# Attention's output with its tokens on the partitions, in the banks of the scores

## The chip, the cores and the metric

One core of a Trainium2 chip. The metric is the time of one execution on the device, in microseconds (us). Engines: TensorE (PE in the profile, PEld its weight loads), VectorE (DVE), ScalarE (ACT), GpSimd (POOL), SyncE (SP), which issues the DMAs here.

## The reference

```python
# q, k, v, f_logit: (4, 8, 768, 48)
f = 1.0 / (1.0 + np.exp(-f_logit))
for t in range(S):
    state = f[:, :, t, :, None] * state + np.einsum('bhd,bhe->bhde', k[:, :, t], v[:, :, t])
    y[:, :, t] = np.einsum('bhd,bhde->bhe', q[:, :, t], state)
x = y.transpose(0, 2, 1, 3).reshape(B, S, H * D)              # (4, 768, 384)
xn = (x - mean(x)) / np.sqrt(var(x) + 1e-06) * g_ln
x = x + np.maximum(xn @ w_ch1, 0.0) @ w_ch2                    # first MLP, 384 - 1536 - 384
h = np.maximum(x.transpose(0, 2, 1) @ w_tok1, 0.0) @ w_tok2    # token mixing, 768 - 256 - 768
u = x + h.transpose(0, 2, 1)
out = u + np.maximum(u @ w_ch1b, 0.0) @ w_ch2b                 # second MLP
```

## The kernel before

Attention with a gate per channel is cut into 24 units: unit n is chunk c = n // 4 (128 tokens) of batch b = n % 4. Gates become cumulated logs (`clamp`, `log`, `scan`), with which k and q are scaled (`ek`, `eq`, `km`, `qm`). A chunk is two halves of 64 tokens (index i), its 8 heads are 4 pairs (index p) of two (index r): head (p, r) has its 48 channels on partitions 64r to 64r + 47 of the tiles K and Q. Most of a unit's products use a quarter of TensorE's array (64 rows by 64 columns). All of them are fp32, and each shows in the trace as two instructions.

The steps of a unit, by their names in the order list:
- `kp` transposes K (4 transposes), `kt` copies it out.
- `sc` (L331): 16 score products (p, r, i), into two PSUM banks, one for each r. `st` (L344): 16 statistics products (new state of each half), into other columns of the same two banks.
- `A0`, `A1` (L354): VectorE masks the scores of r = 0 and r = 1 into A.
- `stm`, `ste`, `std`: state at the middle and the end of the chunk, and its decay.
- `y` (L399): output products that go to PSUM bank k from row half k of the array: 8 `carried(0)` products (old state by Q, first half; only if c > 0) and 8 `inner(0)` (V by A). `yw` (L409): a one-element VectorE memset that waits for the last of `y`. `z` (L416): 8 `inner(1)` and 8 `carried(1)`, whose first waits for that memset, since now the other row half writes each bank. The result `yT` has channels on partitions and tokens along the row.
- `yc0`, `yc1` (L423): ScalarE copies the two banks out. `yt` (L433): 4 transposes turn the output to tokens on partitions.
- `lna`, `lnc`, `lnv`, `lnr`: layer norm from those (`lna` ScalarE, copy with row sums; `lnc` VectorE, centred and scaled xn).
- `tp`: 3 transposes of xn; `ah` (ScalarE) and `al` (VectorE) split them in two fp32r parts.

The first MLP (`mlp`) works in 8 steps of 3 units. `m<step>.<f>` is a first-layer product group (9 products of 128x128 by 384 columns, three terms of a split), `h` (ScalarE) and `l` (VectorE) bring its hidden part out, `o<u><g>` is a second-layer group of 9 products, `r` adds the result to x. Nine such products are a slot. Step s begins at slot 29 + 24 s. Unit n (from 3 on) is placed at s0 = 22 + 8 (n - 3), so one unit goes with eight slots. Steps `w..` convert the first MLP's weights (`a`, `b`, `c` VectorE, `h` ScalarE, `l` VectorE or GpSimd), `s..` those of later stages.

What sets the order: each engine runs its instructions in the order in which they are emitted. Everything due before slot 77 is emitted in the order written out in `ORDER` ("+k" puts k small products on zeros in front, to keep the clock up), the rest sorted by due time, at equal times engines first and TensorE's pieces last, attention before the MLP. `POOL` names the steps that go to GpSimd in place of VectorE; from unit 12 on all that can go there do.

PSUM before: `scp` two banks (scores of one unit), `atp` three (kp, yT, y, tp), `mmp` three (first and second layer products).

Of the kernel before, what the change touches and what calls it, by code (L numbers as in the profile page):

```python
# [7 lines left out]
F32 = mybir.dt.float32  # L8
# [10 lines left out]
DM = H * D  # L19
# [27 lines left out]
    w3.l 2.qm 3.km 3.qm w12.l 1.std 4.qm w14.l w4.l w1.l w5.l 6.km w13.l w17.l w15.l 2.std 5.std 4.std 7.km 3.std  # L47
    w6.l 8.km 8.qm 9.qm w19.l w23.l 11.km 11.qm 11.std
""".split())
ORDER = """  # L50
    0.lf 1.lf 0.clamp 0.log 3.lf w3.ld 4.lf 1.clamp 3.clamp 0.scan 1.log 2.lf 3.log 0.lq 1.lq 1.scan w3.a 2.clamp
    4.clamp 1.ek 3.scan 0.eq 0.lv 0.ek 4.log w12.ld 0.km 2.log w3.b 0.kp+31 0.qm 1.km 0.sc+7 2.scan 0.kt 3.eq
    w14.ld w3.c w3.h 0.st 4.scan 0.A0 0.y+21 w2.ld 1.kp 2.ek 1.eq 1.kt 1.tot 4.ek 0.stm 0.A1 w12.a 0.ste 0.yw 1.lv
    w14.a 1.qm 2.lq 0.tot w3.l w14.b 0.z 0.yc0 1.sc+4 3.tot 2.eq 0.yc1 2.tot 2.qm w12.b 1.st w2.a 2.km 2.kp+5 2.kt
    1.A1 1.A0 1.stm 1.ste w14.c 1.y+3 3.lq 2.lv 0.yt 4.lq 3.ek 3.km 0.lna 5.lf w2.b 2.sc 1.yw 3.lv 0.lnc w2.c
    w0.ld 1.z 2.st 1.yc0 3.qm 2.A1 2.A0 4.tot 0.tp w5.ld 2.stm w4.ld 1.yc1 3.kp 0.ah 3.kt 4.eq 4.lv 0.al w2.h
    2.ste w12.c 2.y+9 6.lf 2.yw 1.yt w2.l 5.clamp 4.km 1.lna w13.ld w12.h 3.sc w1.ld 2.z 2.yc0 5.log 3.st 1.lnc
    w12.l 3.A1 3.A0 1.tp+7 1.std 3.stm 4.qm 2.yc1 4.kp 2.yt 1.ah 5.scan 4.kt 1.al 2.lna 2.lnc 3.ste 3.y+14 3.yw
    2.tp 0.lnv 1.lnv 2.ah 3.z w4.a w0.a 6.clamp w4.b 3.yc0 3.yc1 2.al 4.sc 4.st 3.yt 5.lq w4.c 0.std 5.ek w0.b
    m0.3 4.A0 w14.h 3.lna w14.l 4.y 4.A1 4.stm 6.lv w15.ld m0.2 w4.h w0.c 3.lnc 4.ste 6.log 4.yw w0.h w4.l 2.lnv  # L60
    3.tp 5.eq w1.a w5.a 4.z w1.b 5.km 5.lv w1.c w1.h 4.yc0 m0.h2 m0.h3 5.qm w7.ld m0.4 w17.ld 5.kp 6.scan 5.sc
    4.yc1 m0.l2 w1.l 5.kt m0.l3 4.yt 5.st m0.1 6.tot 4.lna 6.lq w5.b w13.a w5.c w0.l 5.tot w13.b 4.lnc 5.A0 w13.c
    3.ah w5.h m0.0 m0.h4 6.ek m0.h0 5.y m0.l4 5.stm m0.h1 w5.l m0.5 5.A1 w13.h w17.a w11.ld w16.ld 7.lf 5.yw m0.l0
    m0.l1 6.eq w15.a 6.km 5.z 6.qm w15.b 5.ste w13.l w17.b 8.lf 8.lv w16.a 5.yc0 m0.h5 5.yc1 3.lnv m0.o00 w16.b
    7.lq 6.kp 4.tp 6.sc 6.kt w17.c w17.h w15.c 5.yt 6.st m0.o10 w16.c 5.lna m0.l5 6.A1 7.clamp w15.h m0.o20 5.lnc
    w17.l w10.ld w16.h 4.ah 5.tp w16.l w15.l w6.ld m0.o11 m0.o21 5.ah 2.lnr 4.al w6.a 5.al 6.A0 2.std 6.y 7.log
    6.stm 7.scan m0.o01 w19.ld 7.ek m0.r21 8.clamp 6.yw 3.al 5.std w10.a 7.tot m0.r11 w10.b m1.2 w7.a 4.std m1.5
    6.ste w7.b 8.log m0.r01 5.lnv 7.eq 6.z m1.h2 7.km w10.c w7.c 9.lf w6.b m1.l2 w6.c 7.qm m1.1 m1.h1 4.lnv m1.h5
# [12 lines left out]
    10.qm 10.kt 11.lq s2.ld 10.sc m1.d0 m0.r23 s0.a 9.yt 10.st m0.o02 11.ek m1.o13 11.eq m0.o03 m0.o12 10.stm
    m1.r13 s1.b 9.std s0.b 10.A1 10.ste 10.A0 7.std m1.d1 m1.o22 10.std m0.d2 m0.o13 m0.r03 m0.r13 s0.c m0.d1 s1.c
    m0.d0 m1.o23 9.lna 8.lnr s0.h 8.std
# [71 lines left out]
def head(p, r):  # L155

    return 4 * (p // 2) + 2 * r + p % 2


def main_path(ctx, tc, q_t, k_t, f_t, v_n, g_rep, w1, w2, wt1, wt2, w3, w4, out, x1_d, f_d, h_d, t_d):  # L160
# [71 lines left out]
    atp = at.enter_context(tc.tile_pool(name="atp", bufs=3, space=PSUM))  # L232
# [17 lines left out]
    def attention(n):  # L250
# [80 lines left out]
        def scores(z=0):  # L331

            t["sc"] = [scp.tile([128, 512], F32, tag="sc", name="sc") for _ in range(2)]
            busy(t["sc"][0], z)
            for p in range(NP):
                for r in range(2):
                    for i in range(2):
                        nc.tensor.matmul(t["sc"][r][half(i), HC * p:HC * p + HC], t["K"][rows(r), p, half(i)],  # L338
                                         t["Q"][rows(r), p, half(i)])

        def new(i):
            return t["sc"][i][:P2, NP * HC:NP * HC + NP * D]

        def stat():  # L344
            for p in range(NP):
                for i in range(1 if last else 2):
                    for r in range(2):
                        h, w = head(p, r), width(r)
                        o = NP * HC + D * p
                        nc.tensor.matmul(t["sc"][i][64 * r:64 * r + w, o:o + D],  # L350
# [3 lines left out]
        def scores_e(g):  # L354
            a = s2.tile([128, NP, HC], F32, tag=f"A{g}", name=f"A{g}")
            t["A", g] = a
            nc.vector.tensor_tensor(
                a, t["sc"][g][:, :NP * HC].rearrange("p (a c) -> p a c", a=NP),
                upper.rearrange("p (o c) -> p o c", o=1).to_broadcast([128, NP, HC]), op=ALU.mult)
# [20 lines left out]
        def carried(i):  # L380
# [18 lines left out]
        def outp(z=0):  # L399
# [4 lines left out]
            if c:  # L404
                carried(0)
# [10 lines left out]
        def outp2():  # L416
# [3 lines left out]
            carried(1)  # L420
            follow(block.instructions[z], t["done"])

        def outp_e(k):  # L423


            if not k:
# [920 lines left out]
```

## Time and profile before

| | us |
|---|---|
| median of 3 runs | 772.51 (771.8 to 772.72) |
| the profiled execution | 774.89 |
| its span, first to last instruction | 773.1 |
| TensorE busy | 758.7 (98%) |
| VectorE busy | 519.3 (67%) |
| ScalarE busy | 370.4 (48%) |
| GpSimd busy | 147.7 (19%) |
| moved by DMA | 120.18 MB, 155 GB/s |

The granted clock of TensorE is 0.995 of full speed over the span. The start is the attention of the first units and the conversion of weights; from about 41 us the first MLP runs, mixed with attention to about 382 us; then token mixing and the second MLP.

### The profile page before, as it was taken

The numbers are of one execution on the slowest core, as the hardware profiler recorded it, in microseconds if no ns is written. First come the engines' busy times: TensorE is split into PE (matmuls) and PEld (weight loads), VectorE is DVE, ScalarE is ACT, GpSimd is POOL, SyncE is SP. The second block draws the span as 40 slices with busy tenths as digits, with TensorE's granted clock in tenths as the row PEclk, the third lists the DMA queues.
The fourth block names the chain that finished last, engine by engine and source line by source line (L and its number), as shares of the span: only waits on it lengthen the run. The fifth ranks groups of instructions, "written<-read, shape, count | busy, mean of one in ns | idle before, by whom it ended". The sixth has DMA issues, their size and how long they took to land.

```text
span 773.1 us, 17492 instructions
## 1 busy us (share of the span) xinstructions
PE 758.7 (98%) x7110; PEld 735.6 (95%) x7110; DVE 519.3 (67%) x969; ACT 370.4 (48%) x899; POOL 147.7 (19%) x119
## 2 busy tenths in 40 slices
PE   8899999999999999999999999999999999999996
PEld 7799999999999999999999999999999999999996
DVE  7798886687785867555344664877558664868481
ACT  6675454363644645444131442664247442656440
POOL 1344212145343333230000010101001010101010
PEclk9999999999999999999999999999999999999998
DMA  9674342465566555652347984345343544343401
GB/s 264 188 212 157 115 151 68 146 191 193 181 220 171 157 166 171 192 176 84 102 140 272 341 299 139 97 138 170 95 130 93 178 127 137 96 143 100 132 21 67
DMA packets 61001, 120.18 MB, mean 155 GB/s; under 512 B 6896, under 2 KB 29040, under 8 KB 60144
## 3 DMA queue, kind: packets, MB, share of 16 engines
q1 hardware_dynamic: 60912, 118.98, 49.1%
q8 instruction: 58, 0.95, 0.5%
q14 instruction: 31, 0.25, 0.1%
HBM read 94.57 MB, written 24.38 MB: 154 GB/s over the span
## 4 chain that ended last, share of the span: by engine, by line
PE 90%; DMA 3%; DVE 2%; issue 2%; POOL 1%; SPq 1%; ACT 1%; POOLq 0%
PE mo L945 19%; PE mo L576 18%; PE mm L546 18%; PE mm L892 17%; PE rt L812 3%; PE ht L834 3%; PE yT L396 2%; DMA first<-in_q_t 2%; PE yT L387 2%; PE sc L338 2%; PE sc L350 1%; PE y L439 1%; PE tp L510 1%; DMA ts<-t_d 1%; PE kp L315 1%
## 5 line engine op out<-in xcount | busy, mean ns | idle before, releaser
L546 PE MATMUL mm<-wx 128*128 128x384 f32 x864 | 163.2, 340 | 0.4 <-DVE hl L565 0.4
L546 PEld LDWEIGHTS mm<-wx 128*128 128x128 f32 x864 | 148.5, 188 | 2.5 <-DVE hl L565 1.1
L892 PE MATMUL mm<-xsh,wx 128*128 128x384 f32 x528 | 137.9, 334 | 0.9 <-DVE q L908 0.9
L576 PE MATMUL mo<-w2h,hh 128*128 128x384 f32 x288 | 101.1, 351 | 0.2 <-DVE hl L565 0.2
L945 PE MATMUL mo<-w2h,hh 128*128 128x384 f32 x288 | 97.0, 337 | 0.0
L892 PEld LDWEIGHTS mm<-xsh,wx 128*128 128x128 f32 x528 | 95.6, 188 | 1.3 <-PE mm L892 1.2
L576 PE MATMUL mo<-w2h,hl 128*128 128x384 f32 x288 | 96.6, 335 | 0.0
L576 PE MATMUL mo<-w2l,hh 128*128 128x384 f32 x288 | 96.4, 335 | 0.0
L945 PE MATMUL mo<-w2h,hl 128*128 128x384 f32 x288 | 96.3, 334 | 0.0
L945 PE MATMUL mo<-w2l,hh 128*128 128x384 f32 x288 | 96.2, 334 | 0.0
L932 POOL TENSOR_TENSOR hl<-u,hh 128x768 fp32r<-128x768 f32 x16 | 29.7, 1854 | 337.9 <-ACT u L927 244.0
L892 PE MATMUL mm<-xsl,wx 128*128 128x384 f32 x264 | 88.2, 334 | 0.0
L561 ACT ACTIVATE hh<-mm 128x384 fp32r<-128x384 f32 x96 | 46.3, 487 | 62.3 <-PE mm L546 61.7
L565 DVE SCALAR_TENSOR_TENSOR hl<-mm,hh 128x384 fp32r<-128x384 f32 x96 | 52.5, 551 | 22.8 <-ACT hh L561 22.1
L949 DVE TENSOR_TENSOR xr<-mo,xr 128x384 f32<-128x384 f32 x48 | 26.6, 555 | 53.5 <-PE mo L945 53.5
L1103 ACT ACTIVATE cs<-cs 128x384 f32<-128x384 f32 x56 | 31.1, 555 | 59.2 <-DVE cs L1100 59.0
L576 PEld LDWEIGHTS mo<-w2h,hh 128*128 128x128 f32 x288 | 54.1, 188 | 1.9 <-DVE hl L565 0.3
L576 PEld LDWEIGHTS mo<-w2l,hh 128*128 128x128 f32 x288 | 54.2, 188 | 0.0
L945 PEld LDWEIGHTS mo<-w2h,hh 128*128 128x128 f32 x288 | 54.1, 188 | 0.1
L945 PEld LDWEIGHTS mo<-w2l,hh 128*128 128x128 f32 x288 | 54.1, 188 | 0.0
L945 PEld LDWEIGHTS mo<-w2h,hl 128*128 128x128 f32 x288 | 54.1, 188 | 0.0
L576 PEld LDWEIGHTS mo<-w2h,hl 128*128 128x128 f32 x288 | 54.0, 188 | 0.0
(163 smaller groups left out, 1372.7 us busy)
## 6 DMA issues: line engine op xcount, KB each, us to landing
cs<-in_w SPq DMA_DIRECT2D x48, 384.0 KB, 3.3
sg<-in_w SPq DMA_DIRECT2D x44, 384.0 KB, 4.5
ts<-t_d SPq DMA_DIRECT2D x48, 256.0 KB, 2.9
wx<-f_d SPq DMA_DIRECT2D x6, 1152.0 KB, 12.4
F<-in_f_t SPq DMA_DIRECT2D x21, 224.0 KB, 3.9
T<-in_k_t SPq DMA_DIRECT2D x21, 224.0 KB, 3.3
T<-in_q_t SPq DMA_DIRECT2D x21, 224.0 KB, 4.2
x_d<-x SPq DMA_DIRECT2D x24, 192.0 KB, 2.6
```

The lines of the kernel that those rows point to most:

```text
L338: nc.tensor.matmul(t["sc"][r][half(i), HC * p:HC * p + HC], t["K"][rows(r), p, half(i)], t["Q"][rows(r), p, half(i)])
L546: nc.tensor.matmul(ps, w[:, f, k, :], x[:, k, :], start=(i == 0), stop=(i == 8))
L561: nc.scalar.activation(out=hid(f)[0], in_=t[f], func=AF.Relu)
L565: nc.vector.scalar_tensor_tensor(hl, t[f], 0.0, hh.bitcast(F32), op0=ALU.max, op1=ALU.subtract)
L576: nc.tensor.matmul(ps, x, w[:, f, :], start=(f == lo and i == 0), stop=(f == hi and i == 2))
L812: nc.tensor.matmul(t["r"][j], w, x, start=(s == 0 and i == 0), stop=(s == NCH - 1 and i == 2))
L834: nc.tensor.matmul(ps, w, x[:, j], start=(i == 0), stop=(i == 5))
L892: nc.tensor.matmul(ps, w, x, start=n == 0, stop=n == len(ops) - 1)
L932: le.tensor_tensor(l, whole(g, i), h.bitcast(F32), op=ALU.subtract)
L945: nc.tensor.matmul(ps, x, w[:, f], start=(g % 3 == 0 and m == 0 and n == 0), stop=(g % 3 == 2 and m == 1 and n == 2))
L949: nc.vector.tensor_tensor(us[b, u], t["o", u], us[b, u], op=ALU.add)
L1103: nc.scalar.activation(out=t["u"], in_=t["u"], func=AF.Abs, accum_out=wlow[:, i:i + 1])
```

## The change

The heads are paired anew (head (p, r) = 4 r + p), and the output is made with A or Q as the stationary operand and V or the state as the streamed one, so that tokens come out on partitions. It is written into the columns of the unit's own score banks that the scores have left. Bank r then holds the 192 channels of heads 4r to 4r + 3. `yc0`, `yc1` and `yt` go; `lna` and `lnc` read the score banks. For r = 1 the token halves of A are swapped, so V is also loaded with swapped halves (W, half a V more for each unit). `y` is now the 16 inner products, `z` the carried ones behind the memset. The score tile is two banks, two deep; `atp` has one bank (kp); `tp` goes to `mmp`. `ORDER` and `POOL` are written anew.

```diff
 def head(p, r):
-    return 4 * (p // 2) + 2 * r + p % 2
+    return NP * r + p
...
-    atp = at.enter_context(tc.tile_pool(name="atp", bufs=3, space=PSUM))
+    atp = at.enter_context(tc.tile_pool(name="atp", bufs=1, space=PSUM))
...
-                t["V"] = vp.tile([128, DM], F32, tag="V", name="V")
-            nc.sync.dma_start(out=t["V"], in_=v_n[n])
+                v = vp.tile([128, DM + DM // 2], F32, tag="V", name="V")
+                t["V"], t["W"] = v[:, :DM], v[:, DM:]
+                nc.sync.dma_start(out=v, in_=v_n[n])
...
-            t["sc"] = [scp.tile([128, 512], F32, tag="sc", name="sc") for _ in range(2)]
-            busy(t["sc"][0], z)
+            t["sc"] = scp.tile([128, 2, 512], F32, tag="sc", name="sc")
+            busy(t["sc"][:, 0], z)
...
-                        nc.tensor.matmul(t["sc"][r][half(i), HC * p:HC * p + HC], t["K"][rows(r), p, half(i)],
+                        nc.tensor.matmul(t["sc"][half(i ^ r), r, HC * p:HC * p + HC], t["K"][rows(r), p, half(i)],
                                          t["Q"][rows(r), p, half(i)])
...
-                    o = slice(64 * (p % 2), 64 * (p % 2) + width(p % 2))
-                    nc.tensor.matmul(t["yT"][r ^ i][o, r, p // 2], s[rows(r), D * p:D * p + width(p % 2)],
-                                     t["Q"][rows(r), p, half(i)], start=(i == 0 and p < 2),
-                                     stop=(i == 1 and p > 1))
-
-        def inner(r):
+                    nc.tensor.matmul(t["sc"][half(i), r, D * p:D * p + D], t["Q"][rows(r), p, half(i)],
+                                     s[rows(r), D * p:D * p + D], start=False, stop=p == NP - 1)
+
+        def inner():
             for p in range(NP):
-                for i in range(2):
-                    h = head(p, r)
-                    o = slice(64 * (p % 2), 64 * (p % 2) + width(p % 2))
-                    nc.tensor.matmul(t["yT"][r ^ i][o, r, p // 2], t["V"][half(i), D * h:D * h + width(p % 2)],
-                                     t["A", r][half(i), p], start=(c == 0 and r == 0 and p < 2), stop=False)
+                for r in range(2):
+                    for i in range(2):
+                        k = half(i ^ r)
+                        o = D * p
+                        nc.tensor.matmul(t["sc"][half(i), r, D * p:D * p + D], t[r][k, p],
+                                         t["W" if r else "V"][k, o:o + D], start=p == 0,
+                                         stop=p == NP - 1 and c == 0 and i == 0)
...
-            if c:
-                carried(0)
-            inner(0)
+            inner()
             t["half"] = nc.cur_bb.bb.instructions[-1]
...
-            inner(1)
+            if c:
+                carried(0)
             carried(1)
             follow(block.instructions[z], t["done"])
...
-            xn, g = (a.rearrange("p (i a c) -> p i a c", i=4, a=2) for a in (t["xn"], gln))
-            y = t["y"].rearrange("p (i a c) -> p i a c", i=4, a=2)[..., :D]
-            nc.vector.scalar_tensor_tensor(xn, y, t["nm"][:, 0:1], g, op0=ALU.add, op1=ALU.mult)
+            nc.vector.scalar_tensor_tensor(heads(t["xn"]), y(), t["nm"][:, 0:1], heads(gln), op0=ALU.add, op1=ALU.mult)
...
-                (-6, sl.e, ktrans_e, "kt"), (-4.7, sl.p, scores, "sc"), (-4.7, sl.p, stat, "st"),
-                (-4, sl.e, lambda: scores_e(0), "A0"), (-4, sl.e, lambda: scores_e(1), "A1"),
+                (-6, sl.e, ktrans_e, "kt"), (-4.9, sl.p, scores, "sc"), (-4.89, sl.p, stat, "st"),
+                (-4, sl.e, (lambda: scores_e(0)) if n < 11 else scores_e2, "A0"),
+                (-4, sl.e, (lambda: scores_e(1)) if n < 11 else None, "A1"),
...
-                (3, sl.p, outp, "y"), (3.05, sl.e, outp_w, "yw"), (3.2, sl.p, outp2, "z"),
-                (4, sl.e, lambda: outp_e(0), "yc0"), (4, sl.e, lambda: outp_e(1), "yc1"),
-                (5, sl.p, outp_t, "yt"), (6, sl.e, ln_a, "lna"), (7, sl.e, ln_c, "lnc"), (11.1, sl.p, trans, "tp"),
+                (3.01, sl.p, outp, "y"), (3.05, sl.e, outp_w, "yw"), (3.2, sl.p, outp2, "z"),
+                (4.2, sl.e, ln_a, "lna"), (5, sl.e, ln_c, "lnc"), (11.3, sl.p, trans, "tp"),
...
-        ps = atp.tile([128, 512], F32, tag="at", name="tp")
+        ps = mmp.tile([128, 512], F32, tag="mm", name="tp")
```

TensorE's pieces in the two hand-written lists, from unit 4's `y` on ([k] is k groups of nine large products; before it, units 0 to 3 go to `z` and the scores and statistics of unit 4 are done in both; before also has `3.yt`):

```
before: 4.y [1] 3.tp 4.z [1] 5.kp 5.sc 4.yt 5.st [2] 5.y [1] 5.z [1] 6.kp 4.tp 6.sc 5.yt 6.st [2] 5.tp [2] 6.y [3]
        6.z [2] 7.kp [1] 7.sc [1] 7.st [3] 6.yt [2] 8.kp [1] 7.y [1] 8.sc [1] 8.st [1] 7.z [1] 8.y [3] 7.yt 8.z [2]
        6.tp 9.kp [2] 8.yt 7.tp [1] 8.tp 9.sc [1] 9.st [2] 9.y [1] 10.kp 9.z [1] 10.sc 9.yt 10.st [7]
after:  4.y [2] 4.z [2] 5.kp [1] 5.sc 5.st 3.tp 6.kp 4.tp 5.y 6.sc [1] 6.st [2] 5.z [2] 5.tp 6.y [4] 6.z [1] 7.kp
        [1] 7.sc [2] 7.st [4] 7.y [5] 7.z [1] 8.sc [3] 8.kp [2] 8.st 9.kp [1] 6.tp [1] 8.y [1] 8.z 9.sc [1] 7.tp 9.st
        [2] 9.y [1] 8.tp 10.kp 10.sc 9.z [2] 10.st [5]
```

In front of the first large product the new list has these more on VectorE: two weight steps `a`, two `b`, one `c`, both masks of unit 4, two products `qm`; and these less: one `std`, one `l`.

## Rows read from the trace of the kernel before

**Rows 1.** Busy time by stretch, from and to in us.

```profile
142.00:388.00 246.00, 245.41 (x2934) 235.65 (x2933) 168.23 (x332) 117.19 (x291) 79.46 (x61) 1.00 0.54 169
...
424.00:773.00 349.00, 341.80 (x1990) 340.14 (x1988) 223.59 (x366) 165.06 (x392) 29.66 (x16) 0.99 0.45 140
```

The columns are length, then busy us (and instructions) of PE, PEld, DVE, ACT, POOL, then TensorE's granted clock, DMA share and GB/s.

**Rows 2.** TensorE's waits over the span: us in total, times, longest.

```profile
PE sc L338 <- issue: 3.0, 2, 1.6
...
PE mm L546 <- DVE hl L565: 0.4, 1, 0.4
```

**Rows 3.** The chain that ended last: start us, us, what.

```profile
40.85 1.58 PE mm L546 x9
```

**Rows 4.** Busy time by stretch, the start; columns as in rows 1.

```profile
0.00:25.00 25.00, 20.77 (x349) 18.00 (x350) 18.90 (x43) 15.93 (x33) 5.77 (x12) 1.00 0.86 239
25.00:50.00 25.00, 22.90 (x533) 20.36 (x533) 20.76 (x48) 17.68 (x51) 8.10 (x7) 0.93 0.66 210
```

**Rows 5.** Timeline of TensorE, 262 to 290 us: start us, us, what.

```profile
261.67 2.07 PE L546 MATMUL mm<-wx 128*128 128x384 f32 x11
263.67 0.45 PE L387 MATMUL yT<-T,state 48*64 48x64 f32 x16
263.94 0.41 PE L396 MATMUL yT<-A,V 64*48 64x64 f32 x16
264.28 0.45 PE L576 MATMUL mo<-w2h,hh 128*128 128x384 f32 x1
264.57 0.34 PE L576 MATMUL mo<-w2l,hh 128*128 128x384 f32 x1
...
265.78 0.34 PE L576 MATMUL mo<-w2h,hl 128*128 128x384 f32 x1
265.96 0.49 PE L510 MATMUL tp<-ident,xn 128*128 128x128 f32 x3
266.38 0.45 PE L396 MATMUL yT<-A,V 64*64 64x64 f32 x16
266.65 0.41 PE L387 MATMUL yT<-T,mid 48*48 48x64 f32 x16
266.88 0.65 PE L338 MATMUL sc<-T 48*64 48x64 f32 x32
267.34 0.64 PE L350 MATMUL sc<-V,kt 64*48 64x48 f32 x32
267.91 0.44 PE L576 MATMUL mo<-w2h,hh 128*128 128x384 f32 x1
268.19 0.33 PE L576 MATMUL mo<-w2l,hh 128*128 128x384 f32 x1
...
269.60 0.55 PE L439 MATMUL y<-ident,ys 112*128 112x112 f32 x4
269.92 0.42 PE L576 MATMUL mo<-w2h,hh 128*128 128x384 f32 x1
270.17 0.34 PE L576 MATMUL mo<-w2l,hh 128*128 128x384 f32 x1
```

**Rows 6.** The output's transposes, 56 to 390 us: duration ns min/median/max, first and last start.

```profile
L439 PE MATMUL y<-ident,ys x76: 257/259/316, 59.1 to 365.7; 112*128 112x112 f32 x76
```

**Rows 7.** Statistics instructions begun by 267.68 us, by shape: xcount, busy us, mean ns.

```profile
L350 PE MATMUL sc<-V,kt 64*48 64x48 f32 x16 | 0.5, 206 | 0.0
L350 PE MATMUL sc<-V,kt 64*64 64x48 f32 x12 | 0.5, 216 | 0.0
```

**Rows 8.** The copies of xn's transposes, 56 to 390 us, columns as in rows 6.

```profile
L532 DVE TENSOR_TENSOR wx<-tp,wx x21: 544/548/557, 62.4 to 377.8; 128x384 fp32r<-128x384 f32 x21
L528 ACT ACTIVATE wx<-tp x20: 470/491/498, 61.3 to 377.3; 128x384 fp32r<-128x384 f32 x20
```

**Rows 9.** Timeline of VectorE, 195 to 217 us; idle before, in brackets.

```profile
201.98 0.75 DVE L357 TENSOR_TENSOR A<-sc,upper 128x256 f32<-128x256 f32 x2 [2.89 <-PE sc L350]
...
212.47 1.47 DVE L633 TENSOR_TENSOR sg<-cu,sg 128x256 fp32r<-128x256 f32 x1
```

More of the change, by code (lines that the diff above doesn't have):

```diff
@@ L52 @@
[L52 to L56, printed above, removed]
@@ L349, in stat, with scores_e, scores_e2 @@
                         o = NP * HC + D * p
[L350 removed]
+                        nc.tensor.matmul(t["sc"][64 * r:64 * r + w, i, o:o + D],
                                          t["kt"][half(i), P2 * p + 64 * r:P2 * p + 64 * r + w],
                                          t["V"][half(i), D * h:D * h + D])
[L354 to L356 removed]
+        def scores_e(g, gs=None):
+            if g not in t:
+                t["A"] = s2.tile([128, 2, NP, HC], F32, tag="A", name="A")
+                t[0], t[1] = t["A"][:, 0], t["A"][:, 1]
+            g = slice(g, g + 1) if gs is None else gs
+            w = g.stop - g.start
             nc.vector.tensor_tensor(
[L358 to L359 removed]
+                t["A"][:, g], t["sc"][:, g, :NP * HC].rearrange("p r (a c) -> p r a c", a=NP),
+                upper.rearrange("p (r a c) -> p r a c", r=1, a=1).to_broadcast([128, w, NP, HC]), op=ALU.mult)
+        def scores_e2():
+            scores_e(0, slice(0, 2))
         def old():
@@ L418, in outp2, with heads, y @@
             z = len(block.instructions)
-            inner(1)
+            if c:
+                carried(0)
             carried(1)
             follow(block.instructions[z], t["done"])
-        def outp_e(k):
-            if not k:
-                t["yf"] = s1.tile([P2, 10, HC], F32, tag="ys", name="ys")
-                t["ys"] = t["yf"][:, :8].rearrange("p (r g i) c -> p r g (i c)", r=2, g=2)
-            to = t["yf"].rearrange("p (r x) c -> p r x c", r=2)[:, :, 0:3:2] if not k else \
-                t["yf"][:, 1:7].rearrange("p (r x) c -> p r x c", r=2)[:, :, 0:3:2]
-            nc.scalar.activation(out=to, in_=t["yT"][k][:P2], func=AF.Copy)
-        def outp_t(z=0):
-            t["y"] = atp.tile([128, 512], F32, tag="at", name="y")
-            busy(t["y"], z)
-            for g in range(2):
-                for r in range(2):
-                    i = 128 * (2 * g + r)
-                    nc.tensor.matmul(t["y"][:, i:i + P2], t["ys"][:, r, g], ident[:P2, :P2], is_transpose=True)
+        def heads(x):
+            return x.rearrange("p (r c) -> p r c", r=2)
+        def y():
+            return t["sc"][:, :, :DM // 2]
         def ln_a():
@@ L1185, in general_path @@
                         nc.vector.tensor_copy(ya[:, :, :, e], ps)
-                    nc.sync.dma_start(
-                        out=x_d[b].rearrange("c t (p e) -> t c p e", p=NP)[:, :, bass.ds(p, 1), :].rearrange(
-                            "t c p e -> t c (p e)"),
-                        in_=ya.rearrange("t c r e -> t c (r e)"))
+                    for r in range(2):
+                        nc.sync.dma_start(
+                            out=x_d[b].rearrange("c t (h e) -> t c h e", h=H)[:, :, bass.ds(p + NP * r, 1), :].rearrange(
+                                "t c h e -> t c (h e)"),
+                            in_=ya[:, :, r])
         with tc.tile_pool(name="gw", bufs=1) as gw, tc.tile_pool(name="gx", bufs=2) as gx, \
```

84 lines of the change are left out of this document (45 added, 39 removed).

## The prediction

> **What bounds the kernel now.** I read the table of stretches first. From 142 to 388 us, where attention and the first MLP run mixed, TensorE is busy 245.41 of 246 us; behind 424 us it is 341.80 of 349 [rows 1]. VectorE is at 168 of 246 there, ScalarE at 117, the DMA share is 0.54. Then the waits of TensorE: in the whole span it waited 0.4 us for the lower halves of the hidden layer, and 3.0 us for its own instructions near the start [rows 2]. So from about 41 us, where the first product of the first weights starts [rows 3], TensorE has work back to back, and a us that it is spared there is a us off the end, as long as nothing else begins to wait. Before that it is not the bound: VectorE is busy 18.90 and 20.76 of 25 us, DMA at a share of 0.86 and 0.66 [rows 4]. What the change does in this start is costed apart.
>
> A busy TensorE is not one at its peak, so the price of a piece is read as what it inserts between the starts of large products. Their pitch is 0.173 us (264.57 to 265.78 is seven of them); eleven begin at 261.67, so the last at 263.40. One unit of attention, in order of time [rows 5]:
> - Run A (the carried and inner products of the first half, 16 in all): 263.40 to 264.57 less two pitches, 0.82 us. In it, 0.27 us go to entering with the first eight (263.67 to 263.94).
> - Run B (three transposes of xn, the other 16 output products, scores and statistics of the next unit): 265.78 to 268.19 less two pitches, 2.06 us. Inside it the output products take 0.27 and 0.23 us a set of eight, scores 0.46, statistics 0.57 with the way back to whole-array work.
> - The four transposes of the output: 269.60 to 270.17 less one pitch, 0.40 us.
>
> **The change, part by part.** *Transposes of the output out.* 76 of them lie behind 56 us [rows 6], so 19 units, at 0.40: **-7.6 us**. The two ScalarE copies that fed them go too; they stood on an engine with half of its time free [rows 1], so nothing for those.
>
> *One run in place of two.* Behind slot 77 the order is by due time: y(n) at 3.01 behind the product of slot 3, then scores (3.10) and statistics (3.11) of n+1, then z(n) (3.2), then the transposes of xn (3.3), all in front of slot 4. That is one quarter-array run. Built from rows 5: entry 0.27; sixteen inner products 0.50 (0.27 and 0.23; they stream 48 columns now for 64, but hold 64 columns of stationary data, and the statistics with 48 against 64 streamed are no faster than scores, so I give them nothing); scores 0.46; statistics 0.47; z 0.46 if it goes at the rate of the old output products; leaving 0.10; three transposes and the first two starts behind them 0.25 and 0.26; less two pitches: 2.42 us. A and B were 2.88, so 0.46 saved for each of the 13 units 10 to 22: **-6.0 us**. In the part ordered by hand (to slot 77) y and z are still apart: units 4 to 10 come in 20 quarter-array runs by the new list, 22 by the old; each entry and exit is about 0.35 us: **-0.7 us**.
>
> *z has a new order inside.* Before, each eight carried products alternated between the two column halves. Now the eight of half 0 come first, then the eight of half 1. One half alone takes a product each 0.058 us (16 scores in 0.46, two halves at a time). If the halves run one after the other, z costs 0.93 for 0.46; with units 5 to 23 that is 8.9 us. If the second half may start past waiting products of the first, it costs nothing. The nearest row speaks for passing: the statistics are issued in turn, one for output columns 0 to 63, one for 64 to 127; at 267.68 us all 16 instructions of the 48-wide half had begun, but only 12 of the 64-wide half [rows 7]. So a half runs ahead by two products (four instructions), with no sign of a brake; z would need up to eight. Between 0 and 8.9 I take a fifth, nearer to the row: **+1.9 us**. The Trainium skill's page "TensorE: Matmul & The Clock Gate", section "The mechanism", says that matmuls start and end strictly in program order, and only weight loads are pulled ahead. The trace disagrees: 16 against 12 begun. By that rule the sum would have +8.9 here; it is a rival below.
>
> *The score tile is two banks, two deep; the transposes of xn move into the three banks of the large products.* The transposes now end the run, and their ScalarE copy (0.49 us) stands in the queue in front of the copy of the product before the run; behind it VectorE has the lower part of the transposes (0.55) and then that of the product, about as long [rows 8]. 1.59 us and the hops, about 1.8, after the transposes the bank of that product comes free; the next but one product wants it after one product of 1.56 and 0.08. So 0.2 us of wait where the run falls among first-layer products, each third unit, 5 of them: **+1.0 us**. Below, 0 if the hops are short; above, the longest VectorE operation here, 1.47 us, for each of 19 units. Among second-layer products a bank serves 36 products and nobody waits. VectorE has room for it: it idles 2.89 us in one piece in front of A0, for TensorE [rows 9].
>
> *The wait between y and z* (a VectorE memset behind y) was covered by nine large products; now by scores and statistics alone, 0.93 us. Behind z in TensorE's queue stands everything. The memset waits in VectorE's queue behind whatever is running; 1.47 less 0.93 is 0.54 us for the worst, 13 units, so 0 to 7; its usual operation of 0.55 us is shorter than the cover, so I take 0.05 each: **+0.7 us**.
>
> *Start, loads, POOL list.* V brings 0.1 MB more a unit, hidden by DMA at 0.54 from 142 us, not in the start. The new list puts some seven more VectorE operations (weight conversions, masks, two products) in front of the first large product; at 0.55 each [rows 8] that is 3.8 us later if VectorE is the bound there, given back before the first second-layer product, where both lists have done the same work to within one operation. The shorter path per unit (no copies, no transposes) may repay it. From 0 to 3.8 I take **+1.5 us**. Units 0 to 3 have only the second eight carried products, in one half; that lies in the start too. GpSimd is busy 79 of 246 us [rows 1] and takes the steps newly listed for it for nothing.
>
> Sum: -7.6 - 6.0 - 0.7 + 1.9 + 1.0 + 0.7 + 1.5 = **-9.2 us**. Against the profiled execution's 774.89 us that is 765.7; against the median of 772.51, 763.3.
>
> **Rivals.** *z in program order.* For it: nothing shows a half passing eight products. Against: rows 7. 8.9 for 1.9: 763.3 + 7.0 = 770.3. Chance 0.17.
>
> *z wholly side by side, and both waits hidden*: -14.3 + 1.5, 759.7. Chance 0.18.
>
> *The first large product 3.8 us later and not given back*: 765.6. Chance 0.07.
>
> *Inner products slowed by sharing banks.* Before, a bank took results from one row half of the array at a time. Now bank r takes them from row half r for tokens 0 to 63 and from the other for tokens 64 to 127, in one run. No row shows this. If the two halves took turns, the inner products would cost 0.93 for 0.46, for 20 units 9.4 us: 772.7, no change. Chance 0.07. The Trainium skill's page "TensorEngine Tiling (Array Packing)", section "Gotcha 1: PSUM Pressure", says that different row tiles cannot use one PSUM bank at the same time; no run here shows it, and the output partitions differ.
>
> *Slower: the large products wait for a bank that a transpose holds.* Place: the second product behind each run. If al comes one VectorE operation later (0.55 on top of 0.2), 0.75 us for 19 units is 14.3 instead of 1.0: 776.6. It decides from about 0.6 us each. For it: the bank pool is three as before, with a tenant more, and VectorE has operations of 1.47 us [rows 9], and one such stretch already cost TensorE its 0.4 us. Against: only 0.4 us in all. Chance 0.09.
>
> **How the numbers follow.** The forecast itself has 0.42; its own range is 760 to 767 (down by 1.9 for z and 1.7 for the two waits at nothing; up by start and waits at twice my values, 3.2). With the others: faster by more than 0.2% (1.5 us, about what this measurement can tell from none) 0.42 + 0.18 + 0.17 + 0.07 = 0.84; within 0.07; slower 0.09. The range of 759 to 771 holds the first four cases, 0.84.
>
> **What would show it.** Starts inside z: eight products of each half side by side in 0.46 us, or in 0.93. One run per unit of about 2.4 us between large products behind 145 us, and none of the output's transposes [rows 5]. TensorE waits: some tenths at the product behind the transposes for lower halves, none for the memset. The first large product between 40 and 45 us. The number is wrong if TensorE waits for banks or the memset for several us, if z is serial, or if the start moves by more than 4 us. The stages behind attention should keep their length.

## The result, and the profile after

The changed kernel takes **781.93 us** (median of 4 runs, 780.61 to 784.17); the kernel before took 772.15 beside it (771.52 to 772.72). The ratio is 1.013, 95% interval 1.0102 to 1.0158: slower by 1.3%, where 763.3 and a gain were forecast. The profiled execution took 782.92 us, its span is 781.2 (773.1 before).

I first cut both spans at four marks that any timeline shows: the first large product, the first product of step m2 (where the list written by hand ends), the first product of the stage behind the first MLP, and the first product of the second MLP's second layer. Stage lengths in us:

| kernel | start | by hand | by due time | token mixing | rest | span |
|---|---|---|---|---|---|---|
| before | 40.6 | 101.4 | 246.1 | 70.3 | 314.7 | 773.1 |
| after | 47.5 | 99.5 | 247.1 | 72.1 | 315.0 | 781.2 |

So two things went wrong. The start is 6.9 us longer. And the part by due time, where most of the gain was to be made, is 1.0 us longer instead of some 9 shorter. (Token mixing lay between 70.0 and 72.2 in all profiles of this study, with the same code. Here TensorE waits 1.4 us for one DMA in it, `few_fillers` below waits 0.2 at the same line and has 70.6 with all of the change; so the 1.8 isn't the change's.)

Busy time of the two stretches that answer to [rows 1], same columns:

```profile
147.00:394.00 247.00, 240.10 (x2879) 231.96 (x2878) 169.53 (x315) 106.86 (x262) 78.26 (x63) 1.00 0.55 174
430.00:781.00 351.00, 343.85 (x2000) 341.26 (x1998) 224.35 (x367) 166.15 (x394) 29.65 (x16) 1.00 0.44 141
```

TensorE is busy 5.3 us less than in [rows 1], in a stretch 1 us longer: the work did go, and idle time of 6.90 us (0.59 before) came for it. TensorE's waits over the whole span name it (against [rows 2]):

```profile
PE mm L537 <- DVE hl L556: 4.9, 5, 1.4
PE sc L411 <- DVE A L362: 2.9, 2, 1.9
PE kp L495 <- ACT kt L322: 1.9, 1, 1.9
PE sc L495 <- DVE first L448: 1.6, 1, 1.6
...
PE kp L317 <- POOL T L305: 1.0, 1, 1.0
...
PE mo L567 <- DVE hl L556: 0.8, 1, 0.8
PE sc L394 <- DVE done L418: 0.7, 2, 0.5
```

The first, fifth and sixth lie in the part by due time. In the first, large products wait for lower halves of the hidden layer: 0.4 us in one wait before, 4.9 in five now. The second to fourth lie in the start. The wait for the memset (`done`), which I had feared, is 0.2 us behind 147 us.

One unit, in TensorE's timeline (it answers to [rows 5]):

```profile
253.74 1.03 PE L537 MATMUL mm<-wx 128*128 128x384 f32 x5
254.70 0.68 PE L403 MATMUL sc<-V,A 64*64 64x48 f32 x32
255.20 0.66 PE L340 MATMUL sc<-T 48*64 48x64 f32 x32
255.68 0.63 PE L352 MATMUL sc<-V,kt 64*64 64x48 f32 x32
256.13 0.47 PE L394 MATMUL sc<-state,T 48*64 48x48 f32 x10
256.38 0.26 PE L394 MATMUL sc<-mid,T 48*64 48x48 f32 x2
...
256.59 0.46 PE L394 MATMUL sc<-mid,T 48*64 48x48 f32 x10
256.98 0.55 PE L501 MATMUL tp<-ident,xn 128*128 128x128 f32 x3
257.29 4.93 PE L537 MATMUL mm<-wx 128*128 128x384 f32 x27
263.57 0.79 PE L537 MATMUL mm<-wx 128*128 128x384 f32 x3 [1.36 <-DVE hl L556]
```

The run is one, as forecast: inner products (`L403`, 0.50 us to the next group), scores (0.48), statistics (0.45), z (`L394`, 0.85), transposes. It inserts 2.69 us (starts of the large products around it, less one pitch) in each of nine units with the same count of instructions, between 155 and 290 us. Three product groups later TensorE stands for 1.36 us.

The queues of ScalarE and VectorE behind that run. ScalarE first:

```profile
253.24 0.49 ACT L552 ACTIVATE hh<-mm 128x384 fp32r<-128x384 f32 x1 [1.07 <-PE mm L537]
257.57 0.49 ACT L519 ACTIVATE wx<-tp 128x384 fp32r<-128x384 f32 x1 [3.84 <-PE tp L501]
257.95 0.62 ACT L288 ACTIVATE F<-F 112x512 f32<-112x512 f32 x1
258.61 0.63 ACT L289 ACTIVATE F<-F 112x512 f32<-112x512 f32 x1
259.15 0.47 ACT L552 ACTIVATE hh<-mm 128x384 fp32r<-128x384 f32 x1
259.52 0.48 ACT L440 ACTIVATE x<-sc 128x384 f32<-128x384 f32 x1
...
260.23 0.60 ACT L451 ACTIVATE xn<-x,nm 128x384 f32<-128x384 f32 x1
...
260.83 0.51 ACT L623 ACTIVATE sg<-cu 128x384 fp32r<-128x384 f32 x1
261.25 0.47 ACT L552 ACTIVATE hh<-mm 128x384 fp32r<-128x384 f32 x1
```

VectorE, same stretch:

```profile
259.65 0.56 DVE L556 SCALAR_TENSOR_TENSOR hl<-mm,hh 128x384 fp32r<-128x384 f32 x1 [1.00 <-ACT hh L552]
...
261.31 1.29 DVE L293 TENSOR_TENSOR_SCAN F<-seg,F 112x512 f32<-112x512 f32 x1
262.53 0.53 DVE L624 TENSOR_TENSOR sg<-cu,sg 128x384 fp32r<-128x384 f32 x1
262.98 0.54 DVE L556 SCALAR_TENSOR_TENSOR hl<-mm,hh 128x384 fp32r<-128x384 f32 x1
```

ScalarE stands idle for 3.84 us in front of its copy of the transposes (`ah`), since they come last in the run. The two logarithm steps and the copy of the product *before* the run (259.15) are queued behind `ah`; the copy of the product *behind* it, done on TensorE by about 259, comes at 261.25, after two steps of the layer norm (`L440`, `L451`) and a weight conversion (`L623`); VectorE's lower half of that one comes at 262.98, behind a scan of 1.29 us, and ends at 263.52. There are three banks, one of them lent to the transposes. Three product groups behind the run start in one row of 27; the fourth starts at 263.57, when that lower half is read out.

### The profile page after: what moved, and what is told of

Same layout as the page of the kernel before. It is cut to its first block, busy times and chain, and to the rows that moved or that the text cites. A ratio compares the mean times of both kernels' runs of the same rounds, so it can differ in the third digit from the quotient of the medians.

```text
span 781.2 us, 17469 instructions
## 1 busy us (share of the span) xinstructions
PE 756.5 (97%) x7129; PEld 735.0 (94%) x7129; DVE 516.9 (66%) x950; ACT 355.2 (45%) x851; POOL 152.9 (20%) x125
## 4 chain that ended last, share of the span: by engine, by line
PE 86%; DVE 4%; DMA 3%; issue 2%; ACT 2%; POOL 1%; SPq 1%; POOLq 0%; DVEq 0%
PE mo L936 19%; PE mo L567 18%; PE mm L883 16%; PE mm L537 15%; PE rt L803 3%; PE ht L825 3%; PE sc L394 2%; PE sc L403 2%; DMA ts<-t_d 1%; PE sc L340 1%; PE sc L352 1%; PE tp L501 1%; PE kp L317 1%; PE tp L837 1%; DMA F<-in_f_t 1%
## 5 line engine op out<-in xcount | busy, mean ns | idle before, releaser
L537 PE MATMUL mm<-wx 128*128 128x384 f32 x864 | 161.5, 339 | 4.9 <-DVE hl L556 4.9
L567 PE MATMUL mo<-w2h,hh 128*128 128x384 f32 x288 | 99.0, 344 | 1.0 <-DVE hl L556 0.8
L936 PE MATMUL mo<-w2h,hh 128*128 128x384 f32 x288 | 97.0, 337 | 0.0
```

Source lines behind the costliest of these rows:

```text
L537: nc.tensor.matmul(ps, w[:, f, k, :], x[:, k, :], start=(i == 0), stop=(i == 8))
L567: nc.tensor.matmul(ps, x, w[:, f, :], start=(f == lo and i == 0), stop=(f == hi and i == 2))
L936: nc.tensor.matmul(ps, x, w[:, f], start=(g % 3 == 0 and m == 0 and n == 0), stop=(g % 3 == 2 and m == 1 and n == 2))
```

## The experiments

All runs, beside runs of the kernel before on the same chip in the same session. There were four sessions (the first four rows, the next four, the three `z_tp` rows, the three with `mid`), so across them the ratios compare, not the medians. Medians in us; each ratio is to the kernel before, with its interval (1.0130 [1.0102, 1.0158] for the changed kernel); the last columns are the stages of the profiled execution.

| kernel | median (range, runs) | ratio | start | by hand | by due |
|---|---|---|---|---|---|
| z_turns | 779.22 (775.84–781.15, 4) | 1.0076 [1.0054, 1.0099] | 47.9 | 98.1 | 243.1 |
| tp_ahead | 775.71 (772.19–777.56, 10) | 1.0014 [0.9995, 1.0033] | 49.7 | 100.0 | 240.0 |
| few_fillers | 780.78 (776.08–783.01, 6) | 1.0090 [1.0073, 1.0107] | 42.8 | 100.4 | 247.1 |
| ln_late | 779.55 (777.83–781.06, 4) | 1.0071 [1.0046, 1.0095] | 46.7 | 99.5 | 245.2 |
| all_three | 768.99 (766.70–773.65, 10) | 0.9940 [0.9917, 0.9962] | 47.6 | 97.6 | 236.9 |
| no_fillers | 779.15 (one run) | – | 42.6 | 102.4 | 247.1 |
| old_start | 786.70 (785.91–790.17, 4) | 1.0174 [1.0141, 1.0206] | 51.6 | 101.2 | 247.1 |
| old_start_two | 775.11 (772.35–778.93, 12) | 1.0019 [1.0000, 1.0038] | 52.5 | 99.8 | 236.4 |
| z_tp | 769.99 (766.55–774.22, 12) | 0.9956 [0.9935, 0.9976] | 53.0 | 97.9 | 236.4 |
| z_tp_y | 769.75 (766.85–771.00, 6) | 0.9951 [0.9931, 0.9970] | 48.5 | 98.6 | 236.7 |
| z_tp_kp | 768.04 (765.98–770.72, 6) | 0.9941 [0.9922, 0.9960] | 43.4 | 98.0 | 237.0 |
| mid_ahead | 783.20 (781.26–788.95, 6) | 1.0127 [1.0096, 1.0159] | 49.2 | 100.1 | 247.1 |
| z_tp_mid | 770.24 (767.77–772.40, 8) | 0.9960 [0.9942, 0.9978] | 46.0 | 98.2 | 236.6 |
| z_tp_kp_mid | 768.42 (766.25–771.43, 7) | 0.9940 [0.9918, 0.9962] | 45.3 | 97.6 | 236.8 |

**z_turns: the two column halves of z by turns again.**

```diff
-        def carried(i):
-            s = t["S"][1] if i else old()
             for p in range(NP):
+                for i in range(0 if c else 1, 2):
+                    s = t["S"][1] if i else old()
                     for r in range(2):
```

> The carried products of z go through the two column halves in turn again, as in the kernel before; all else is the changed kernel. Theory A (z one half after the other stands on the path): z falls from 0.85 us with its way out to about 0.57, 0.3 us for each of 20 units, 5.5 to 6 us: about 776, still slower than before by some 4. Theory B (TensorE waits for the hidden layer's lower halves anyway, and z only fills those waits): less than 2 us, the waits for them grow from 4.9 us by what z gives up.

The run inserts 2.40 us for 2.69, 0.29 less, fourteen times; the part by due time is 4.0 shorter, the part by hand 1.4. z from its first instruction to the transposes takes 0.66 us for 0.85. The waits stay, as the last lines of the same stretch show:

```profile
254.36 4.93 PE L536 MATMUL mm<-wx 128*128 128x384 f32 x27
260.65 3.65 PE L536 MATMUL mm<-wx 128*128 128x384 f32 x18 [1.35 <-DVE hl L555]
```

So z's order costs 5.4 us of the span, and it has nothing to do with the waits. The median, 779.22, is above the 776 that I expected; its four executions had a granted clock of 0.989 to 0.994 over the span, where the changed kernel's had 0.993 to 0.997.

**tp_ahead: the transposes of xn in front of the run, not at its end.**

```diff
-                (4.2, sl.e, ln_a, "lna"), (5, sl.e, ln_c, "lnc"), (11.3, sl.p, trans, "tp"),
+                (4.2, sl.e, ln_a, "lna"), (5, sl.e, ln_c, "lnc"), (11.005, sl.p, trans, "tp"),
```

> Behind slot 77 the transposes of xn stand in front of y at the head of the quarter-array run, not at its end; z stays as in the changed kernel. Theory A (ScalarE stands still for the whole run in front of the copy of these transposes, and the copies of the large products queue behind it): the five waits of 0.85 to 1.5 us some four products behind a run fall to 0.3 or less each, 4 to 5 us in all: about 777.5. Theory B (a bank of the large products too few): the transposes then hold a bank for longer, so the waits stay or grow: 782 or more.

The part by due time falls by 7.1 us, to 240.0, more than the 4 to 5 expected. The lines of the same unit, TensorE:

```profile
253.63 0.49 PE L501 MATMUL tp<-ident,xn 128*128 128x128 f32 x3
254.05 0.68 PE L403 MATMUL sc<-V,A 64*64 64x48 f32 x32
...
256.34 5.99 PE L537 MATMUL mm<-wx 128*128 128x384 f32 x32
```

and ScalarE:

```profile
252.27 0.49 ACT L552 ACTIVATE hh<-mm 128x384 fp32r<-128x384 f32 x1 [1.07 <-PE mm L537]
254.16 0.49 ACT L519 ACTIVATE wx<-tp 128x384 fp32r<-128x384 f32 x1 [1.40 <-PE tp L501]
...
255.74 0.47 ACT L552 ACTIVATE hh<-mm 128x384 fp32r<-128x384 f32 x1
...
258.21 0.49 ACT L552 ACTIVATE hh<-mm 128x384 fp32r<-128x384 f32 x1
```

ScalarE stands 1.40 us for 3.84, the copy of the product before the run comes 1.7 us after the run's first inner product for 4.45, and 32 large instructions follow without a wait. The transposes hold their bank longer here than in the changed kernel (their lower half is read through 257.3, with 253.63 as their start). A bank merely lent to them is therefore not what makes the large products wait; the copies that queue behind `ah` are.

**ln_late: `lna` and `lnc` later** (due times 4.2 and 5 to 6 and 7, and unit 9's `lnc` out of the hand-written list), to take ScalarE's copies of x out of the way of the hidden layer's.

> Behind slot 77 the two copies of the layer norm (ScalarE and VectorE) are due 1.8 and 2 slots later, as in the kernel before; all else is the changed kernel. Theory A (ScalarE's standstill before the transposes' copy causes the waits): the waits stay above 3 us in all, less than 1.5 us gained. Theory B (the earlier layer norm, 0.88 us of ScalarE and 0.61 of VectorE in front of the next lower half, causes them): the five waits fall by half or more, 3 us gained, about 779.

The part by due time is 1.9 us shorter, between the limits of the two theories and a small part of the 7.1; 3.4 us of waits stay, in seven. These copies add to the queue; they don't set it.

**few_fillers and no_fillers: the products on zeros in the start.** In the changed kernel's list they stand in two long rows in front of work that VectorE waits for. The lines of the changed kernel:

```profile
16.65 4.60 PE L495 MATMUL kp<-zeros 128*128 128x224 bf16 x29 [1.86 <-ACT kt L322]
...
41.34 3.68 PE L411 MATMUL sc<-zeros 128*128 128x64 bf16 x72 [1.91 <-DVE A L362]
```

The second row is new in kind: y's products on zeros go into the score tile now, so they wait for VectorE's A (1.91) and run behind it. Before they went into the output's own tile, not that of the scores; a line of that kernel, with no wait in it:

```profile
27.29 1.03 PE L504 MATMUL yT<-zeros 128*128 128x224 bf16 x9
```

few_fillers cuts both rows short; no_fillers takes every product on zeros out of the list (56 in front of everything stay).

```diff
-    w14.b 1.km 4.scan 3.ek 0.lv 0.tot 2.eq 0.kt w2.a 3.eq w12.a w2.b w12.b w14.c 3.tot 2.lq w14.h w2.c 1.kp+29
+    w14.b 1.km 4.scan 3.ek 0.lv 0.tot 2.eq 0.kt w2.a 3.eq w12.a w2.b w12.b w14.c 3.tot 2.lq w14.h w2.c 1.kp+5
...
-    w1.h 3.st w4.h 1.ah 3.A1 3.A0 4.kp 6.lf 2.lnc w3.h 4.kt 3.y+24 w0.ld 2.tp 4.sc 2.ah 1.lnv 4.st 3.stm 1.al
+    w1.h 3.st w4.h 1.ah 3.A1 3.A0 4.kp 6.lf 2.lnc w3.h 4.kt 3.y+4 w0.ld 2.tp 4.sc 2.ah 1.lnv 4.st 3.stm 1.al
```

> Two counts of products on zeros in the hand order are cut: in front of unit 1's transposes of K 5 for 29, in front of unit 3's y 4 for 24 (three small ones each). Theory A (these fillers stand on the path: 72 small ones took 3.68 us while VectorE idled 3.88 for TensorE, the 29 took 4.6): the first large product moves from 47.5 us to 42.5 to 44, 3.5 to 5 us less in all. Theory B (they stand where TensorE would wait for VectorE or for loads anyway, and keep its clock up): the start ends as before within 1 us, or later by what a half clock costs.

> The changed kernel with no products on zeros in the hand order at all (the 56 in front of everything stay). If they only fill waits, the start is 47.5 us or longer by a lower clock; if they stand on the path, it is below the 42.8 us of the run with two of them cut, unless the clock falls for more than it did (0.93 in each of the first two stretches of 25 us).

The profiled start is 4.6 us shorter for few_fillers, as theory A has it, but the median only 1.2 us below the changed kernel's (measured in another session; 1.0090 for 1.0130 by the ratios). The six executions tell why. The profiled one is one of the two shortest: 776.08 and 776.75 us, at a granted clock of 0.994 and 0.997 over the span. The other four took 780.77 to 783.01, at 0.984 to 0.987. The changed kernel took 780.61 at 0.997 and 782.92 at 0.994. So the cut does shorten the path, by 4 to 7 us at an equal clock, and where the gain is gone, the granted clock is lower. The rows of the whole start are of the profiled executions, so the row of few_fillers doesn't show that loss. Before, after, few_fillers, no_fillers, in this order:

```profile
0.00:40.62 40.62, 34.29 (x714) 30.00 (x715) 30.28 (x68) 26.05 (x62) 9.34 (x15) 0.96 0.74 215
```

```profile
0.00:47.48 47.48, 38.74 (x814) 34.33 (x814) 30.33 (x70) 25.66 (x59) 11.22 (x17) 0.93 0.68 203
```

```profile
0.00:42.84 42.84, 32.43 (x729) 28.39 (x729) 30.35 (x70) 25.63 (x59) 11.28 (x17) 0.96 0.74 222
```

```profile
0.00:42.63 42.63, 30.84 (x597) 26.14 (x598) 31.19 (x72) 26.18 (x60) 11.42 (x17) 0.68 0.77 225
```

With no products on zeros left in the list, the clock stood at its lower level, 1.2 GHz, for 27 of 42.6 us. And VectorE has the same work in all four starts, 30.3 to 31.2 us: what differs is how long it stands.

**all_three: z by turns, transposes ahead, both rows cut.**

> The three edits together on the changed kernel: z in turns, the transposes of xn at the head of the run, 5 and 4 products on zeros for 29 and 24. If the three causes are apart (start, z, ScalarE's standstill), their gains by stage add: start 43 us for 47.5, behind slot 77 some 236.5 us for 247.1, the rest as it was: a span of 763 to 765, about 765 beside 773 of before. If z and the waits for the lower halves are one thing (z in turns only moves the wait), 3 to 4 us less is gained: 768 to 769.

768.99 us, 0.6% below the kernel *before*. That is the number of the second theory, but the stages are those of the first: the gains of the first two edits add (by due 236.9, by hand 97.6). What is missing is the start, 47.6 us again, at a granted clock of 0.78.

**old_start and old_start_two: the list of before up to the first large product**, with the new steps in the old places and the GpSimd list of before for them; the second also with z by turns and the transposes ahead.

> The changed kernel with the list of before up to the first large product (without the copies and transposes that are gone; the layer norm's copies in their places; unit 0's second mask ahead of its y), then the new list. Theory A (the new list's start is what costs 7 us): first large product at 39 to 42 us for 47.5, 5 us less or more. Theory B (the new form of the output costs the start, whatever the list: both masks and the whole of y in front of the wait): 45 us or later, less than 2.5 us gained.

> The old list's start with the two edits behind it (z in turns, transposes of xn at the head of the run). Start as in the run with the old start alone, the stage behind slot 77 some 236.5 us: if the old start is 40 to 42 us, a span of 761 to 763.

The start is 51.6 and 52.5 us, longer than with the new list, at granted clocks of 0.81 and 0.82; VectorE is busy 36 us in it. But something else ends this start. In old_start TensorE is through with the attention's pieces at 46.7 us and then waits for ScalarE's conversion of a weight (4.2 us of this in old_start_two):

```profile
PE mm L506 <- ACT wx L193: 4.9, 1, 4.9
```

So the old list, taken over like this, is no cure. It doesn't clear the new list either: whether that as such lengthens the start, these two runs don't show. The rest of the second kernel repeats z_tp.

**z_tp, z_tp_y, z_tp_kp: the first two edits together; then with only 3.y's, or only 1.kp's, products on zeros cut.**

> z's column halves by turns and the transposes of xn ahead of the run, nothing else; the products on zeros stay as in the changed kernel. If the two gains add: hand-ordered part 98, due-ordered part 236.5 to 237, start 47.5 as in the changed kernel, span 781.2 - 5.4 - 7.1 = 768.7. Theory A (products on zeros stand on the start's path): 4 us above the kernel that also cuts them, so 772 to 773 in the median. Theory B (whatever the cut saves on the path is paid back by the clock): the same as that kernel, 769.

> As the kernel before it, with 4 in place of 24 products on zeros ahead of 3.y. Theory A: start shorter by 20/24 of 3.68 us at the half clock, 3.1, or half of it at the full clock, 1.5; median 1.5 to 3 lower than with them. Theory B: the clock is granted late for the first large products instead, no gain (0 to 1).

> As the first of the three, with 5 in place of 29 products on zeros ahead of 1.kp. Theory A: start shorter by 24/29 of 4.60 us, 3.8 at most, since VectorE waits for TensorE's scores behind them; median 2 to 4 lower. Theory B: the half clock then lasts for most of the first 45 us (about 17 us of it in the kernel that cuts both, 3.4 here), no gain or 1 us worse.

The gains add: 236.4 by due, 97.9 by hand, as expected. z_tp's runs spread over 7.7 us, from 766.55 at a granted clock of 0.999 over the span to 774.22 at 0.990; the last is the profiled one, with a start of 53.0 at 0.87. Cutting 3.y brings 0.2 us in the median, cutting 1.kp 2.0, and the three intervals overlap: neither theory fits both, and which row matters more isn't resolved.

**mid_ahead, z_tp_mid, z_tp_kp_mid: VectorE's copy `mid` in front of y** in units 0, 2 and 3.

```diff
-    1.sc 0.st 0.A0 0.A1 2.km 1.lv 5.lf 0.y+11 0.stm 1.kt w12.c 1.st 2.qm 0.yw 0.z 3.lq 0.ste 1.A1 0.lna 2.lv w14.l
+    1.sc 0.st 0.A0 0.A1 0.stm 2.km 1.lv 5.lf 0.y+11 1.kt w12.c 1.st 2.qm 0.yw 0.z 3.lq 0.ste 1.A1 0.lna 2.lv w14.l
```

In the start VectorE waits for TensorE 12.9 us where it waited 2.6. Its waits in the changed kernel's start:

```profile
DVE mid L377 <- PE sc L403: 6.9, 3, 3.9
DVE A L362 <- PE sc L352: 4.9, 2, 4.4
```

> The changed kernel with the step mid of units 0, 2 and 3 ahead of y in the list; nothing else. Theory C (mid waits for y, whose output lies in the statistics' tile since the change, and holds VectorE's queue): VectorE's waits for y (6.9 us in 3) fall to under 1, y waits 0.35 us longer each time, and the first large product starts 3 to 6 us earlier, at 42 to 44; median 776 to 779. Theory D (that wait lies beside TensorE's own chain, which sets the start): the wait moves to another row of VectorE, start 46 to 48, median 781 to 782.

> The same move on the kernel with z by turns and the transposes ahead. Theory C: 3 to 6 us off its 770.0, so 764 to 767; theory D: 769 to 770.

> The same move on the kernel that has 5 products on zeros in place of 29 ahead of 1.kp as well. Theory C: 2 to 4 us off its 768.0 (the first two of the three waits are 1.9 us each there, the third 2.5), 764 to 766, start 40 to 42. Theory D: 768.

The wait ahead of `mid` is gone, and the time isn't: by their ratios (1.0127, 0.9960, 0.9940) the three are where the kernels without the move are (1.0130, 0.9956, 0.9941). In mid_ahead VectorE still waits for the statistics ahead of A, and now stands at another place; and TensorE waits for `mid`, which it never did in the changed kernel:

```profile
DVE A L362 <- PE sc L352: 4.8, 2, 4.3
DVE wx L523 <- issue: 3.5, 1, 3.5
PE sc L411 <- DVE mid L377: 3.7, 3, 2.3
```

So theory C fell. Statistics, scores and output share a tile now; with y first VectorE's `mid` waits for it, with `mid` first y waits.

**What the starts have in common.** If a start's work runs at the pace of the granted clock, (1 - clock) times its length is what the lower level cost, an upper estimate from the row of the start. Taken off, the changed kernel's start is 47.48 - 0.07 × 47.48 = 44.2 us, and those of the five kernels with the same products on zeros that I compared, z_turns, tp_ahead, ln_late, mid_ahead and z_tp_mid, are 44.6, 44.7, 44.8, 44.3 and 44.2; z_tp's 46.1. With one row cut or both: 41.1 (few_fillers), 41.6 (z_tp_kp), 41.7 (z_tp_kp_mid), 41.7 (z_tp_y). Before: 39.0. For all_three (37.1) and no_fillers (29.0) the estimate takes off too much, as VectorE's 30 us don't follow that clock; the two old starts are left out, since a weight conversion ends them. So by this estimate 1.7 of the 6.9 us are the clock and 5.2 the chain itself, some 3 of them the products on zeros of the two rows. Starts with the same products on zeros lie up to 1.9 us apart by it, so it is rough.

TensorE's own time can be added up without it. What the products on zeros alone take of the start, before and after, in the columns of length, PE, PEld, DVE, clock, DMA share and GB/s:

```profile
0.00:40.62 40.62, 18.87 (x157) 15.91 (x157) 0.15 (x1) 0.96 0.74 215
0.00:47.48 47.48, 25.10 (x272) 22.38 (x272) 0.15 (x1) 0.93 0.68 203
```

They are 272 for 157 (123 of the 272 are small), and keep TensorE busy 6.2 us longer, at a lower clock. Its other work takes 13.6 us for 15.4, and it stands idle 8.7 for 6.3.

The clock changes from execution to execution, and falls where products on zeros go. Over the span, the median of the executions is 0.987 for few_fillers and 0.9945 for the changed kernel, 0.987 for all_three and 0.991 for z_tp_kp and 0.9945 for z_tp; z_tp_y, with 60 small ones cut, has 0.9935.

## Why the prediction was wrong, point by point

**What bounds the kernel** held: from the first large product on, what TensorE was spared came off, and each wait it was given went on.

**The removed work was sized nearly right.** In the part by due time lie 14 units' transposes, 14 × 0.40 = 5.6 us of the 7.6, and the 6.0 for one run in place of two: 11.6. The run was built at 2.42 us without the term for z, by the second start behind it less two pitches. By that measure it takes 2.49 in z_turns (251.78 to 254.62), 0.39 less than the 2.88 before, not 0.46: 5.1 us in 13 units. Together 10.7 for 11.6. z_tp agrees: with z's order and the late transposes mended, that part is 236.4; its stalls (starts of large products, away from a run, that come later than their pitch) are 1.8 us in sum, against 0.2 before. (246.1 - 0.2) - (236.4 - 1.8) = 11.3, of which 1.0 are waits at the runs and at K's transposes that the kernel before had. The part by hand became 1.8 us shorter, 3.2 without z's 1.4; five units' transposes are 2.0 of it, so the new list gave 1.2 for my 0.7. The inner products were no slower for sharing banks (0.50 us for 16), so that rival falls. The Trainium skill's rule cited for it ("TensorEngine Tiling (Array Packing)", section "Gotcha 1: PSUM Pressure"), that different row tiles can't use one bank at once, cost nothing here, where the two row halves write different partitions of a bank in one run.

**z's new order (+1.9) was mis-sized.** It measured 5.4: 4.0 by due time and 1.4 by hand, 0.29 us a unit where a fifth of 0.46 was taken. The timeline shows how much may pass: `mid`, the second half, begins when 10 of the first half's 16 instructions, 5 of its 8 products, have begun. Five products of 0.058 us are 0.29, which fits; no run varied the number. [Rows 7] showed a lead of two products and I read it as "no brake"; a brake at three fits the same rows. The Trainium skill's rule of program order ("TensorE: Matmul & The Clock Gate", section "The mechanism") would have given 0.46 a unit; the trace lies between, since `mid` does begin ahead of `state`'s last instructions.

**The wait behind the run (+1.0) is the step that failed.** I built it from the copies behind the transposes, 1.59 us and the hops, as if nothing else stood in those two queues, and for the bank of the product *before* the run. In the unit shown, that bank is read out at 260.21, 3.2 us after the transposes began where I had 1.8, and nobody waits for it. What counts is the bank of the product *behind* the run, and the engine I had given "half of its time free": ScalarE runs its queue in order, and its copy of late transposes stops everything behind it, 3.84 us here. Two logarithm steps, two steps of the layer norm and a weight conversion then stand ahead of the copy that matters, and a scan ahead of its lower half. What large products start late by due time, at the runs and away from them, sums up to 10.3 us, against 2.5 before: 7.8 more, for 1.7 forecast with the memset. Moving the transposes alone brings that sum back to 2.5, and the part 7.1 us down. I had asked what follows the copy on VectorE, not what queues up on ScalarE *while the copy waits*. The slower rival (776.6) was nearest: a large product does wait for a bank. Its place (the second product) and its releaser (the transposes' own lower half) were wrong.

**The memset (+0.7)**: 0.2 us behind 147 us; it was nearly hidden. GpSimd's extra steps "for nothing": TensorE waited 1.0 us once for one (kp for T).

**The start (+1.5) failed too**: it measured 6.9, beyond the 4 that I had named as a sign of a wrong number. By the first large product VectorE had done two operations more (70 for 68), not seven, with 30.33 us of work against 30.28; it stood still for TensorE. I read the list for what it gave VectorE and did not price the rows of products on zeros in TensorE's queue, one of which now has to wait for A, nor the granted clock of such a start, 0.93 for 0.96. About 2 us of TensorE's longer chain I have not placed; the place of `mid` isn't it, and how the 6.9 split is an estimate. Giving y's products on zeros a tile of their own again wasn't tried: the attention's pool has only one bank now, for K's transposes.

Together: 5.4 more than forecast for the start, 3.5 for z, 6.1 for the stalls (7.8 for 1.7), 0.9 for the removed work less 0.5 for the new list, and 2.0 behind 394 us make 17.4, against 17.2 us between the forecast (765.7 for the profiled execution) and 782.92.

The change was sound, its order wasn't: z_tp_kp, with three small edits, runs at 768.04, 0.9941 [0.9922, 0.9960] of the kernel before. Its profiled execution, 765.98 us with a start of 43.4, is its shortest and has 0.996 for the granted clock over the span; the median has 0.991. So what keeps it from 763.3 is, as far as these rows show, the start and its clock.

## What to carry to other kernels

An instruction that waits costs its engine's whole queue: when a producer moves later, list what stands behind its consumer on *that* engine, however idle it is on average, and follow it to the next buffer. Where a start is a chain between two engines, cost the padding products and the clock along with the work, since taking the padding out may only trade one for the other. And a rate read from two neighbours passing each other by two is no rate for eight: bound it by the whole length.

## What the runs showed of the hardware

- In z, products for different column halves of the array passed each other only a short way: with eight products for one half issued ahead of eight for the other, the second half began (256.38) after five of the first, and the run took 0.29 us longer than with the halves by turns.
- ScalarE was busy for 107 of 247 us, and yet its copies that waited for late transposes (3.84 us in the unit shown) cost TensorE 7.1 us in the part by due time; with the transposes ahead of the run that wait was 1.40 us, and TensorE had none behind it.
- Taking products on zeros away made single starts up to 4.6 us shorter and the medians 0.2 to 2 us lower, as the granted clock over the span fell (0.987 for 0.9945 with both rows cut); with none left in the list it stood at 1.2 GHz for 27 of the first 42.6 us. Profiled starts of kernels with the very same products on zeros lay between 46.0 us (clock 0.96) and 53.0 (0.87), and runs of one kernel spread by up to 7.7 us, where the kernel before spreads by up to 5.6 (771.32 to 776.9).
